# New issue ranks for the steps of an attention and expert kernel

## Chip, cores and metric

The kernel runs on one NeuronCore of a Trainium2 chip. The metric is the device time of one execution in microseconds (us), lower is better. PE is the matmul engine (TensorE), PEld its weight loads, DVE the vector engine, ACT the scalar engine, POOL is GpSimd, SP the engine that issues most transfers.

## The reference, cut to what matters

```python
# q, k, v: (8 batches, 8 heads, 576, 64) float32
q_d, k_d, v_d = means of q, k, v over groups of 4 positions       # 144 pooled positions
out_up    = repeat(softmax(q_d k_d^T / 8) v_d, 4)                  # pooled attention, every query
out_local = softmax(q k^T / 8, only where |i - j| < 4) v           # local attention
x = (out_up + out_local) as (4608 tokens, 512)
logits = x @ w_gate                                                # 8 experts
# pairs (token, expert) are taken in order of falling logit; a token goes to the first
# expert that still has room (576 tokens each)
for e in range(8):
    out[tokens of e] = relu(x[tokens of e] @ w1[e]) @ w2[e]        # 512 -> 1024 -> 512
```

## The kernel before

The program has two parts, the attention (class `Attention`, from L60) and the experts with their routing (classes `Experts` and `Routing`). Neither is a plain loop. Each part is cut into streams, and each stream is a Python generator whose pieces between two `yield`s are called steps. A planner (class `Plan`) always runs the step with the lowest rank among the next steps of all streams; a step that needs an event which no step has given yet first runs the stream that gives it. What a step runs is appended to the program, so the order of steps is the order of instructions on every engine, and each engine works through its own instructions in that order. The ranks come from a table, `KEYS` (L1484), with one list per stream and one number per step; the two parts share the table and each has its own sequence, 1947 steps for the attention (ranks 0 to 1946) and 1641 for the experts (0 to 1640). The last number of most lists belongs to the empty end of a stream.

The attention's streams, with the batch or unit as the last number of their names:

- `Nq0`, `Nk0`, `Nv0` and so on (`load`, L155): SP loads a batch's q, k or v, 1 MB, in one transfer (two halves for batch 0) into one of six buffers. `Nt` loads the last 16 pooled groups of q and k (two transfers of 128 KB, one buffer, so batch b waits until batch b-1 has been read by step `Q`), `Nw` the same of v (waits until POOL has summed the batch before).
- `Rq000` to `Rk117` (`trw`, L291): PE transposes a quarter of a batch's q or k (L300), ACT or DVE copies it out of the accumulator (L279 and L277 are the helper's lines). `Q0` (`trt`, L323) does the tail groups (L333).
- `Gq00`, `Gk20` (`gsum`, L248): sums over groups of four for the pooled attention, on POOL, for batch 0 on DVE (L266, L269). `U0` (`gsum_v`, L224): the same for v on POOL (L234 to L243).
- `B00` (`down_s`, L354): pooled scores on PE (L362, L365), then maximum and difference on DVE and the exponential on ACT. `C00` (`down_t`, L391): transposes of these weights on PE and the copy out on ACT (L410). `E00` (`down_v`, L414): the products with v and the division; `E1` also writes them to HBM.
- `S_0` to `S_35` (`loc_s`, L487): local scores of four windows of 32 queries (L505, L511), softmax on DVE, ACT and, for the last scaling, POOL (L536). `T_0` (`loc_t`, L540): transposes of these weights (L546) and the copy out on ACT (L554). `W_0` loads the windows of v, `P_0` the pooled result, `V_0` (`loc_v`, L559) multiplies (L569) and copies the rows of x out, `D_0` stores them, `X_0` (`logits`, L591) computes the gate's logits of 128 tokens.
- `F0`, `F1` clear buffers; `F0` also has 13 matmuls that nothing uses. `Z0`, `Z1` prepare the first routing.

The experts' streams, with k, the turn of the expert, as the number: `S` and `R` are the routing of turn k (a chain of small DVE operations and small matmuls that finds the tokens), `L` loads its weights (four transfers of 1 MB on SP, L1283), `W` splits them into two 16-bit parts (a cast on ACT, L1298, and a difference on DVE, L1303; eight pieces of three steps), `G` gathers its tokens' rows (POOL, L1326), `X` splits these and transposes them by DMA (L1367), `H` is the first product on PE (32 steps of 6 matmuls, L1394), `E` the relu (L1422, L1426), `C` the second product (40 steps of 3 matmuls of 512 columns, L1449, in five chunks of eight steps, with two accumulators `pX` in turn) and `Y` the scaling on ACT (L1468) and the scatter to the output (POOL, L1473). A chunk of `C` waits until `Y` has read the chunk two before. Matmuls at L795 and L1340 compute nothing that is used.

Of the kernel before, what the change touches and what calls it, by code (L numbers as in the profile page):

```python
# [1246 lines left out]
class Experts:  # L1247
# [237 lines left out]
    "B00": [48, 52, 67, 69, 546],  # L1485
    "B01": [223, 224, 233, 245, 246],
    "B02": [309, 314, 323, 348, 360],
    "B03": [545, 564, 573, 593, 630],
    "B04": [769, 778, 792, 825, 1726],
    "B05": [1013, 1020, 1047, 1048, 1078],  # L1490
    "B06": [1327, 1329, 1339, 1428, 1431],
    "B07": [1565, 1566, 1573, 1595, 1924],
    "B10": [78, 89, 90, 96, 112],
    "B11": [234, 244, 251, 280, 288],
    "B12": [370, 378, 383, 392, 709],
    "B13": [566, 578, 580, 586, 588],
    "B14": [859, 864, 868, 869, 871],
    "B15": [1052, 1062, 1077, 1112, 1243],
    "B16": [1387, 1390, 1391, 1406, 1522],
    "B17": [1572, 1580, 1589, 1606, 1641],  # L1500
    "B20": [82, 98, 99, 109, 764],
    "B21": [237, 258, 277, 282, 793],
    "B22": [389, 391, 402, 430, 1171],
    "B23": [577, 591, 595, 598, 1911],
    "B24": [875, 897, 910, 917, 1079],
    "B25": [1085, 1091, 1097, 1113, 1277],
    "B26": [1393, 1410, 1412, 1419, 1474],
    "B27": [1579, 1591, 1599, 1614, 1616],
    "C0": [138, 148, 201, 202, 216, 218, 228, 229, 232, 236, 237, 240, 241, 250, 252, 257, 259, 265, 267, 268, 275, 276, 283, 286, 287, 293, 299, 303, 308, 311, 312, 315, 318, 319, 320, 336, 338, 339, 341, 342, 343],
    "C00": [101, 102, 520],  # L1510
    "C01": [305, 321, 1001],
    "C02": [416, 420, 463],
    "C03": [658, 674, 1156],
    "C04": [946, 951, 1374],
    "C05": [1134, 1138, 1306],
    "C06": [1451, 1452, 1462],
    "C07": [1659, 1665, 1746],
    "C1": [386, 399, 400, 417, 437, 438, 447, 448, 454, 464, 470, 471, 474, 476, 483, 486, 491, 494, 496, 507, 511, 516, 518, 521, 527, 528, 533, 536, 540, 541, 546, 548, 553, 554, 555, 565, 570, 576, 577, 578, 579],
    "C10": [125, 128, 429],
    "C11": [331, 337, 585],  # L1520
    "C12": [448, 469, 501],
    "C13": [683, 687, 689],
    "C14": [935, 937, 1517],
    "C15": [1184, 1185, 1885],
    "C16": [1456, 1465, 1631],
    "C17": [1620, 1667, 1841],
    "C2": [604, 632, 647, 669, 670, 674, 678, 679, 694, 695, 704, 705, 715, 716, 720, 721, 723, 729, 730, 734, 735, 738, 742, 747, 750, 754, 755, 758, 760, 761, 767, 769, 781, 782, 783, 784, 794, 795, 796, 797, 798],
    "C20": [116, 117, 133],
    "C21": [304, 310, 312],
    "C22": [457, 462, 786],  # L1530
    "C23": [620, 622, 787],
    "C24": [927, 929, 930],
    "C25": [1126, 1133, 1560],
    "C26": [1448, 1449, 1563],
    "C27": [1656, 1672, 1674],
    "C3": [856, 885, 886, 892, 896, 897, 904, 910, 911, 919, 920, 924, 926, 928, 929, 931, 937, 938, 941, 942, 948, 954, 959, 962, 966, 969, 970, 975, 977, 981, 988, 989, 996, 998, 1000, 1002, 1004, 1007, 1008, 1009, 1010],
    "C30": [118, 122, 126],
    "C31": [294, 296, 332],
    "C32": [483, 485, 1778],
    "C33": [654, 659, 782],  # L1540
    "C34": [940, 941, 1498],
    "C35": [1145, 1149, 1400],
    "C36": [1444, 1447, 1594],
    "C37": [1637, 1646, 1785],
    "C4": [1045, 1093, 1104, 1106, 1111, 1112, 1116, 1123, 1141, 1147, 1148, 1150, 1154, 1155, 1158, 1159, 1166, 1167, 1169, 1173, 1176, 1180, 1181, 1184, 1187, 1192, 1194, 1195, 1196, 1202, 1204, 1210, 1219, 1220, 1222, 1223, 1224, 1225, 1226, 1227, 1229],
    "C5": [1267, 1276, 1278, 1279, 1323, 1325, 1327, 1328, 1331, 1333, 1335, 1336, 1337, 1338, 1339, 1342, 1345, 1346, 1347, 1348, 1353, 1355, 1356, 1357, 1358, 1359, 1360, 1361, 1362, 1363, 1364, 1365, 1368, 1369, 1370, 1371, 1377, 1378, 1380, 1386, 1404],
    "C6": [1413, 1424, 1466, 1468, 1476, 1477, 1478, 1479, 1480, 1481, 1482, 1483, 1489, 1490, 1491, 1499, 1501, 1503, 1504, 1505, 1506, 1507, 1508, 1509, 1513, 1515, 1517, 1520, 1522, 1524, 1525, 1527, 1530, 1531, 1533, 1534, 1535, 1537, 1538, 1539, 1541],
    "C7": [1593, 1594, 1595, 1596, 1597, 1598, 1599, 1600, 1601, 1602, 1603, 1604, 1605, 1606, 1608, 1609, 1611, 1612, 1613, 1614, 1615, 1616, 1617, 1618, 1620, 1621, 1622, 1623, 1624, 1625, 1626, 1627, 1629, 1630, 1631, 1632, 1633, 1634, 1635, 1636, 1640],
    "D_0": [426, 1747],
    "D_1": [403, 1120],  # L1550
    "D_10": [1063, 1322],
    "D_11": [1075, 1698],
    "D_12": [1110, 1618],
    "D_13": [959, 1269],
    "D_14": [1229, 1479],
    "D_15": [1315, 1814],
    "D_16": [1182, 1199],
    "D_17": [1291, 1603],
    "D_18": [1361, 1463],
    "D_19": [1467, 1662],  # L1560
    "D_2": [540, 1738],
    "D_20": [1432, 1476],
    "D_21": [1478, 1615],
    "D_22": [1607, 1925],
    "D_23": [1658, 1839],
    "D_24": [1621, 1675],
    "D_25": [1759, 1897],
    "D_26": [1772, 1834],
    "D_27": [1713, 1865],
    "D_28": [1876, 1928],  # L1570
    "D_29": [1852, 1854],
    "D_3": [671, 1230],
    "D_30": [1843, 1895],
    "D_31": [1860, 1869],
    "D_32": [1898, 1946],
    "D_33": [1919, 1923],
    "D_34": [1881, 1883],
    "D_35": [1921, 1927],
    "D_4": [827, 1418],
    "D_5": [635, 851],  # L1580
    "D_6": [824, 1172],
    "D_7": [780, 1162],
    "D_8": [1014, 1195],
    "D_9": [932, 1002],
    "E0": [121, 124, 128, 140, 145, 157, 166, 172, 180, 187, 194, 203, 208, 222, 230, 231, 235],
    "E00": [148, 150, 151, 164],
    "E01": [341, 343, 358, 397],
    "E02": [511, 512, 513, 680],
    "E03": [694, 699, 701, 722],
    "E04": [965, 969, 970, 971],  # L1590
    "E05": [1204, 1205, 1225, 1399],
    "E06": [1486, 1490, 1492, 1729],
    "E07": [1685, 1686, 1687, 1853],
    "E1": [353, 364, 373, 374, 390, 392, 394, 398, 408, 409, 414, 419, 443, 468, 469, 475, 1329],
    "E10": [152, 154, 155, 156, 157, 158, 159],
    "E11": [342, 362, 365, 367, 368, 376, 395],
    "E12": [529, 549, 551, 554, 559, 603, 604],
    "E13": [761, 762, 763, 772, 800, 801, 806],
    "E14": [988, 1006, 1007, 1008, 1028, 1030, 1239],
    "E15": [1215, 1226, 1228, 1231, 1232, 1256, 1539],  # L1600
    "E16": [1496, 1513, 1514, 1518, 1519, 1521, 1574],
    "E17": [1688, 1701, 1703, 1707, 1708, 1736, 1913],
    "E2": [580, 583, 593, 594, 597, 606, 630, 631, 646, 649, 667, 668, 686, 697, 707, 711, 976],
    "E3": [799, 800, 807, 809, 821, 825, 836, 837, 848, 852, 862, 869, 893, 894, 898, 903, 1161],
    "E4": [1015, 1021, 1025, 1039, 1049, 1057, 1060, 1067, 1072, 1082, 1100, 1103, 1118, 1137, 1144, 1145, 1203],
    "E5": [1232, 1235, 1242, 1243, 1259, 1260, 1263, 1264, 1289, 1290, 1291, 1294, 1299, 1300, 1315, 1317, 1319],
    "E6": [1405, 1406, 1415, 1416, 1417, 1418, 1423, 1425, 1444, 1445, 1451, 1455, 1471, 1472, 1473, 1484, 1485],
    "E7": [1548, 1549, 1554, 1555, 1557, 1558, 1566, 1567, 1573, 1574, 1581, 1582, 1587, 1589, 1590, 1591, 1592],
    "F0": [1, 41],
    "F1": [45, 414],  # L1610
    "G0": [55, 56],
    "G1": [224, 225],
    "G2": [465, 479],
    "G3": [618, 672],
    "G4": [830, 833],
    "G5": [1061, 1168],
    "G6": [1250, 1284],
    "G7": [1427, 1469],
    "Gk00": [43, 51],
    "Gk01": [146, 192],  # L1620
    "Gk02": [250, 269],
    "Gk03": [525, 526],
    "Gk04": [756, 757],
    "Gk05": [934, 936],
    "Gk06": [1275, 1392],
    "Gk07": [1508, 1555],
    "Gk20": [53, 77],
    "Gk21": [186, 214],
    "Gk22": [308, 320],
    "Gk23": [502, 507],  # L1630
    "Gk24": [833, 1353],
    "Gk25": [966, 1190],
    "Gk26": [1301, 1905],
    "Gk27": [1493, 1609],
    "Gq00": [16, 19, 20],
    "Gq01": [123, 130, 303],
    "Gq02": [240, 266, 372],
    "Gq03": [487, 493, 770],
# [519 lines left out]
```

## Time and profile before

| what | value |
|---|---|
| time, median of 3 runs | 694.86 us (691.03 to 695.32) |
| profiled execution: time / span | 698.04 us / 696.40 us |
| PE busy, share of the span | 649.7 us, 93% |
| PEld, DVE, ACT, POOL busy | 468.3, 489.7, 356.0, 252.6 us |
| mean granted clock of PE | 0.990 of full speed |
| attention, routing of the first expert, rest (read from PE's lines) | 0 to 244, 244 to 272, 272 to 696 us |

The span runs from the first to the last instruction of the profiled execution; its time is 1.64 us longer. Busy time of an engine is the union of its instructions; the end of a matmul is modelled. The views used are windows (busy time in given stretches), the chain of waits (followed back from the end), waits (who waited for whom), the timeline of an engine, and groups of instructions by line.

### The profile page before, as it was taken

To read this page: it belongs to the slowest core of one execution; us is meant where nothing else is said; L and a number is where in the kernel's file an instruction comes from. 1 tells how busy PE (TensorE), PEld (TensorE's weight loads), DVE (VectorE), ACT (ScalarE), POOL (GpSimd) and SP (SyncE) were. 2 spreads that over 40 slices of the span, in tenths; PEclk is the share of its full clock that TensorE was granted. 3 is DMA by queue.
4 is the path that set the end of the run, shared out by engine and by line. 5 is a ranking of instruction groups with operands and counts; after the bars stand their busy time and mean duration, and the time that the engine had idled before them with its cause. 6 is when DMAs were issued, how large, how long until landed. Compare 5 with 4: busy or idle time off the path is not lost.

```text
span 696.4 us, 19145 instructions
## 1 busy us (share of the span) xinstructions
PE 649.7 (93%) x7702; PEld 468.3 (67%) x7702; DVE 489.7 (70%) x1408; ACT 356.0 (51%) x711; POOL 252.6 (36%) x330
## 2 busy tenths in 40 slices
PE   6898999899899897998999999989999999999994
PEld 3787789788798866674664665664665764755741
DVE  5888487686777968797998887868986765552300
ACT  5796978968786714334334253234443355342210
POOL 8589747493764305004122131131131212211011
PEclk9999999999999999999999999999999999999997
DMA  9958888868877716339256744624734775431001
GB/s 271 299 124 248 242 235 244 223 195 239 230 197 186 221 40 192 119 126 264 57 207 140 284 129 113 252 82 97 274 92 99 276 216 151 145 60 62 8 32 38
DMA packets 137713, 116.80 MB, mean 168 GB/s; under 512 B 86232, under 2 KB 114392, under 8 KB 137624
## 3 DMA queue, kind: packets, MB, share of 16 engines
q1 hardware_dynamic: 130104, 93.71, 46.3%
q0 software_dynamic: 6512, 21.24, 9.7%
q8 instruction: 61, 1.00, 0.6%
q10 hardware_dynamic: 1008, 0.62, 0.4%
q14 instruction: 28, 0.23, 0.1%
HBM read 86.05 MB, written 21.23 MB: 154 GB/s over the span
## 4 chain that ended last, share of the span: by engine, by line
PE 41%; issue 25%; POOL 11%; DVE 8%; DMA 6%; ACT 6%; SPq 2%; another core or an unknown queue 0%; POOLq 0%; DVEq 0%; ACTq 0%
PE pH L1394 13%; PE pX L1449 13%; POOL out_dram L1473 3%; POOL xg L1326 2%; DMA nat<-in_q_dram 2%; PE o L569 2%; ACT qz L279 2%; DMA x_dram<-x 2%; POOL gtmp L266 2%; PE pR L850 1%; PE g L511 1%; PE g L300 1%; PE pX L795 1%; DMA nat<-in_k_dram 1%; DMA nat<-in_v_dram 1%
## 5 line engine op out<-in xcount | busy, mean ns | idle before, releaser
L1394 PE MATMUL pH<-xt,wh 128*128 128x256 f16 (+1 forms) x1024 | 191.6, 286 | 0.6 <-DVE xt L1354 0.6
L1449 PE MATMUL pX<-wh,ht 128*128 128x512 f16 (+1 forms) x640 | 187.5, 379 | 0.0
L1394 PE MATMUL pH<-xt,wl 128*128 128x320 f16 (+1 forms) x512 | 144.7, 287 | 0.0
L1449 PEld LDWEIGHTS <-ht 128*128 128x128 f16 (+1 forms) x960 | 79.2, 100 | 79.5 <-issue 2.2
L1473 POOL DMA_INDIRECT out_dram<-y,idx x40 | 41.4, 1036 | 213.4 <-ACT y L1468 180.0
L1449 PE MATMUL pX<-wl,ht 128*128 128x512 f16 (+1 forms) x320 | 118.1, 380 | 0.0
L1394 PEld LDWEIGHTS <-wh 128*128 128x128 f16 x1024 | 94.4, 98 | 32.0 <-issue 5.6
L1422 ACT ACTIVATE ht<-pH 128x512 f16<-128x512 f32 (+1 forms) x128 | 45.5, 407 | 136.3 <-PE pH L1394 92.8
L1303 DVE SCALAR_TENSOR_TENSOR wl<-nat,wh 128x512 f16<-128x512 f32 x128 | 84.2, 683 | 12.9 <-ACT wh L1298 12.5
L1426 DVE SCALAR_TENSOR_TENSOR ht<-pH,ht 128x512 f16<-128x512 f32 (+1 forms) x128 | 52.2, 449 | 41.2 <-ACT ht L1422 37.3
L1298 ACT ACTIVATE wh<-nat 128x1024 f16<-128x1024 f32 x64 | 65.9, 1054 | 2.5 <-DMA nat<-in_moe_w_dram 2.5
L1326 POOL DMA_INDIRECT xg<-x_dram,idx x40 | 43.2, 1080 | 62.8 <-DVE idx L1177 33.0
L1468 ACT ACTIVATE y<-pX 128x512 f32<-128x512 f32 (+2 forms) x41 | 23.9, 584 | 79.0 <-PE pX L1449 38.2
L1394 PEld LDWEIGHTS <-wl 128*128 128x128 f16 x512 | 50.1, 98 | 13.0
L554 ACT COPY pt<-g 38x512 f32<-38x512 f32 x72 | 41.7, 579 | 5.4 <-PE g L546 3.4
L569 PE MATMUL o<-vw,pt 128*64 128x64 f32 x1152 | 41.0, 224 | 2.4 <-ACT x L581 1.8
L300 PE MATMUL g<-ident,nat 128*128 128x128 f32 x256 | 36.3, 277 | 7.4 <-DMA nat<-in_q_dram 3.0
L569 PEld LDWEIGHTS o<-vw,pt 128*64 128x64 f32 x1152 | 36.9, 138 | 5.5 <-issue 2.1
L511 PE MATMUL g<-kt,qz 128*64 128x38 f32 x1152 | 40.0, 225 | 0.5 <-ACT kt L279 0.5
L511 PEld LDWEIGHTS g<-kt,qz 128*64 128x64 f32 x1152 | 39.4, 138 | 1.3 <-issue 1.2
L536 POOL TENSOR_TENSOR sw<-sw,rs 128x304 f32<-128x304 f32 x36 | 25.2, 704 | 39.8 <-DVE rs L534 28.2
L266 POOL TENSOR_TENSOR gtmp<-qz 64x576 f32<-64x576 f32 x28 | 32.0, 1143 | 18.5 <-DVE kdt L269 7.3
(234 smaller groups left out, 1145.8 us busy)
## 6 DMA issues: line engine op xcount, KB each, us to landing
nat<-in_moe_w_dram SPq DMA_DIRECT2D x28, 1024.0 KB
vw<-in_v_dram SPq DMA_DIRECT2D x136, 78.0 KB
x_dram<-x SPq DMA_DIRECT2D x36, 256.0 KB
nat<-in_q_dram SPq DMA_DIRECT2D x7, 1024.0 KB
nat<-in_k_dram SPq DMA_DIRECT2D x7, 1024.0 KB
nat<-in_v_dram SPq DMA_DIRECT2D x7, 1024.0 KB
vw<-up_dram SPq DMA_DIRECT2D x36, 64.0 KB
up_dram<-xu SPq DMA_DIRECT2D x8, 256.0 KB
```

Of the source, the lines that this page charges most:

```text
L266: eng.tensor_tensor(tmp.rearrange("p a (w i) -> p a w i", w=NW) if which == "q" else tmp, sv[..., ::2], sv[..., 1::2], op=OP.add)
L300: nc.tensor.transpose(p[:, a, :, fp], src[:, 4 * hh + 2 * a + s, 2 * fp:2 * fp + 2].rearrange("p f d -> p (f d)"), self.ident)
L511: nc.tensor.matmul(sv[64 * a:64 * a + 64, 4 * g + c], self.qz[b % 2][:, 2 * g + a, w].rearrange("p s q -> p (s q)"), self.kt[b][:, 2 * g + ...
L569: nc.tensor.matmul(o[64 * i:64 * i + 64, 64 * (4 * g + h):64 * (4 * g + h) + 64], pt[:, 2 * g + i, h].rearrange("p b q -> p (b q)"), self. ...
L1298: nc.scalar.activation(hi, r, AF.Copy, scale=sc)
L1303: nc.vector.scalar_tensor_tensor(lo[:, a:a + LOP], r[:, a:a + LOP], sc, hi[:, a:a + LOP], op0=OP.mult, op1=OP.subtract)
L1326: self.fetched = self.nc.gpsimd.indirect_dma_start(out=xg[:n], out_offset=None, in_=self.x, in_offset=bass.IndirectOffsetOnAxis(ap=idx[:n, ...
L1394: nc.tensor.matmul(p[:, s, :s1 - s0], self.w[k, d][a][:, 128 * f:128 * f + 128], self.xt[k][:, b, d, s0:s1], start=j == 0, stop=j == len(s ...
L1422: nc.scalar.activation(hi, q, AF.Relu)
L1426: nc.vector.scalar_tensor_tensor(lo, q, 0.0, hi, op0=OP.max, op1=OP.subtract)
L1449: nc.tensor.matmul(p[o:o + m], self.ht[k][:, f, h0:h0 + m], self.w[k, 4 + f // 2][b][:, 512 * (f % 2):512 * (f % 2) + 512], start=j < part ...
L1473: i = nc.gpsimd.indirect_dma_start(out=self.out, in_=y[:n], in_offset=None, out_offset=bass.IndirectOffsetOnAxis(ap=plan.vals["idx", k][:n ...
```

## The change

All lists of `KEYS` are replaced but seven (`G0`, `L0`, `M0`, `R0`, `S0`, `S1`, `G1`); the number of steps in each list is the same, and no other line changes. In the attention the rank of a step moves by 83 in the mean and 37 in the median, in the experts by 12 and 5. The first 99 steps of the experts (the routing of the first expert and the start of its products) keep their ranks. Of the 1126 lines of the diff, these are the ones that the text below speaks of (the new lists follow the old):

```diff
--- before.py
+++ after.py
@@ -1482,568 +1482,568 @@
 ENG = mybir.EngineType
 ORDX = {ENG.PE, ENG.DVE, ENG.Activation, ENG.SP}
 KEYS = {
...
-    "B00": [48, 52, 67, 69, 546],
-    "C05": [1134, 1138, 1306],
-    "C35": [1145, 1149, 1400],
-    "E05": [1204, 1205, 1225, 1399],
-    "Gk00": [43, 51],
-    "H5": [1191, 1201, 1215, 1216, 1228, 1237, 1238, 1239, 1240, 1241, 1245, 1247, 1251, 1253, 1255, 1256, 1262, 1265, 1273, 1274, 1280, 1281, 1282, 1283, 1292, 1293, 1295, 1296, 1297, 1298, 1303, 1306, 1313],
-    "Nk0": [23, 27, 316],
-    "Nk3": [334, 346],
-    "Nk7": [1317, 1318],
-    "Nq0": [7, 11, 647],
-    "Nq5": [734, 738],
-    "Nq7": [1292, 1797],
-    "Nt0": [0, 2],
-    "Nt1": [70, 364],
-    "Nw0": [75, 1003],
-    "Nw2": [333, 555],
-    "Q0": [3, 4, 5, 6, 202],
-    "Q1": [83, 84, 86, 87, 100],
-    "Rk103": [375, 407, 431, 433],
-    "Rq000": [8, 9, 10, 13],
-    "Rq007": [1363, 1369, 1370, 1562],
-    "S_33": [1682, 1722, 1725, 1727, 1730, 1731, 1743, 1766],
-    "T_33": [1771, 1810, 1817, 1877],
-    "W5": [1054, 1066, 1073, 1110, 1117, 1119, 1142, 1153, 1165, 1185, 1199, 1200, 1221, 1246, 1249, 1252, 1254, 1268, 1269, 1271, 1272, 1277, 1285, 1286, 1287],
-    "Y4": [1156, 1175, 1190, 1230, 1231, 1261, 1266],
...
+    "B00": [50, 64, 67, 81, 326],
+    "C05": [1181, 1185, 1722],
+    "C35": [1177, 1182, 1315],
+    "E05": [1211, 1212, 1213, 1261],
+    "Gk00": [42, 130],
+    "H5": [1200, 1226, 1229, 1231, 1232, 1234, 1236, 1238, 1240, 1241, 1243, 1244, 1248, 1261, 1263, 1265, 1266, 1268, 1270, 1271, 1273, 1275, 1278, 1279, 1285, 1290, 1294, 1295, 1300, 1313, 1314, 1316, 1319],
+    "Nk0": [12, 27, 38],
+    "Nk3": [297, 361],
+    "Nk7": [1399, 1821],
+    "Nq0": [2, 26, 1125],
+    "Nq5": [726, 1003],
+    "Nq7": [1116, 1388],
+    "Nt0": [5, 59],
+    "Nt1": [34, 387],
+    "Nw0": [24, 374],
+    "Nw2": [348, 446],
+    "Q0": [8, 11, 15, 16, 23],
+    "Q1": [48, 60, 61, 70, 74],
+    "Rk103": [367, 381, 383, 547],
+    "Rq000": [3, 4, 9, 10],
+    "Rq007": [1237, 1279, 1281, 1403],
+    "S_33": [1694, 1699, 1704, 1705, 1709, 1719, 1738, 1739],
+    "T_33": [1755, 1780, 1795, 1924],
+    "W5": [1058, 1092, 1106, 1137, 1168, 1179, 1193, 1195, 1196, 1197, 1198, 1201, 1202, 1204, 1205, 1206, 1207, 1208, 1209, 1210, 1211, 1212, 1213, 1214, 1215],
+    "Y4": [1142, 1148, 1216, 1217, 1242, 1256, 1262],
...
```

## Rows read from the trace of the kernel before

**Rows 1.** windows: us busy of PE, PEld, DVE, ACT, POOL; clock, DMA share, GB/s

```profile
0.00:25.00 25.00, 18.09 (x195) 12.28 (x195) 16.28 (x32) 14.09 (x25) 16.23 (x23) 1.00 0.96 289
25.00:50.00 25.00, 23.43 (x431) 20.46 (x424) 20.71 (x49) 23.66 (x52) 20.89 (x29) 1.00 0.66 183
50.00:75.00 25.00, 21.65 (x426) 19.55 (x426) 18.46 (x38) 18.95 (x44) 20.92 (x29) 1.00 0.77 226
75.00:200.00 125.00, 116.00 (x2360) 105.59 (x2359) 87.97 (x219) 104.33 (x216) 80.89 (x113) 1.00 0.81 229
200.00:244.00 44.00, 41.25 (x936) 37.52 (x935) 37.65 (x100) 30.23 (x61) 19.54 (x42) 1.00 0.71 203
244.00:272.00 28.00, 25.15 (x288) 18.98 (x284) 18.84 (x82) 7.50 (x11) 4.71 (x7) 0.94 0.32 105
272.00:440.00 168.00, 161.19 (x1305) 101.17 (x1305) 143.03 (x480) 66.60 (x131) 37.85 (x39) 0.99 0.51 155
440.00:470.00 30.00, 27.41 (x249) 20.20 (x246) 23.91 (x73) 11.15 (x24) 8.37 (x9) 1.00 0.56 193
470.00:690.00 220.00, 215.49 (x1536) 132.50 (x1533) 122.84 (x342) 79.48 (x151) 43.16 (x42) 1.00 0.42 123
```

**Rows 2.** chain of waits, 376 to 379 us: start, length, what

```profile
377.24 1.32 PE pX L1449 x6
```

**Rows 3.** timeline of PE, 324 to 463 us: start, length, what, idle before

```profile
325.39 0.31 PE L850 MATMUL pR<-oh,cmp 128*128 128x64 bf16 x5 [1.74 <-DVE thr L833]
...
459.00 0.16 PE L890 MATMUL pR<-un,nohead 128*128 128x1 bf16 x1 [1.52 <-DVE un L877]
...
461.71 0.31 PE L850 MATMUL pR<-oh,cmp 128*128 128x64 bf16 x5 [1.07 <-DVE cmp L808]
```

**Rows 4.** timeline of the SP queue, first 10 us

```profile
0.88 0.69 SPq L167 DMA_DIRECT2D natt<-in_q_dram  x1
1.63 0.57 SPq L167 DMA_DIRECT2D natt<-in_k_dram  x1
2.25 1.13 SPq L195 DMA_DIRECT2D nat<-in_q_dram  x2
```

**Rows 5.** timeline of PE, 8 to 27 us

```profile
9.40 1.09 PE L300 MATMUL g<-ident,nat 128*128 128x128 f32 x8 [1.47 <-DMA nat<-in_q_dram]
...
18.46 0.97 PE L362 MATMUL g<-kdt,qdz 128*128 128x144 f32 x6 [1.99 <-DVE kdt L269]
...
25.20 1.16 PE L333 MATMUL g<-ident,natt 128*64 128x64 f32 x32
```

**Rows 6.** chain of waits, 55 to 67 us

```profile
57.75 0.33 POOL gtv L242
58.08 0.16 SPq L178
...
58.29 6.74 DMA nat<-in_k_dram
...
65.16 0.63 PE g L300 x4
```

**Rows 7.** chain of waits, 176 to 190 us

```profile
178.40 8.05 DMA nat<-in_q_dram
```

**Rows 8.** timeline of PE, 186 to 188 us

```profile
186.58 0.63 PE L300 MATMUL g<-ident,nat 128*128 128x128 f32 x4 [1.16 <-DMA nat<-in_q_dram]
```

**Rows 9.** groups of instructions: busy us, mean ns of one, idle before

```profile
L1298 ACT ACTIVATE wh<-nat 128x1024 f16<-128x1024 f32 x64 | 65.9, 1054 | 2.5 <-DMA nat<-in_moe_w_dram 2.5
...
L266 POOL TENSOR_TENSOR gtmp<-qz 64x576 f32<-64x576 f32 x28 | 32.0, 1143 | 18.5 <-DVE kdt L269 7.3 <-ACT qz L349 5.9 <-DVE qz L277 2.6
...
L410 ACT COPY ptd<-g 128x384 f32<-128x384 f32 (+1 forms) x32 | 13.9, 455 | 1.2 <-PE g L402 0.5 <-PE g L398 0.3
```

**Rows 10.** timeline of PE, 225 to 232 us

```profile
230.29 0.66 PE L546 MATMUL g<-ident,sw 128*128 128x128 f32 x4 [1.24 <-POOL sw L536]
```

**Rows 11.** timeline of DVE, 316 to 330 us

```profile
324.63 0.21 DVE L833 SCALAR_TENSOR_TENSOR thr<-pR,tabs 128x49 int16<-128x49 f32 x1 [2.15 <-remote]
```

1060 rows, old and new, of the table KEYS are left out of this document.

## The prediction

> **What bounds the kernel now.** I read the windows by stretch first, then what PE waits for, then the timelines where it waits. The reader is to see three parts in [rows 1]. In the attention (0 to 244 us) PE is busy 18.09 + 23.43 + 21.65 + 116.00 + 41.25 = 220.4 us, so 23.6 us are idle; a fourth to a third of that lies in the first 25 us, and ACT is close behind (23.66 of 25 us in the second stretch) and POOL too (20.89 and 20.92). From 244 to 272 the routing of the first expert runs as a chain, with PE partly busy on filling matmuls. From 272 on PE is the engine that sets the end: 161.19 of 168, 27.41 of 30, and 215.49 of 220, of which the last 4 us or so are the tail after the last matmul. The work there is dense: six products of 512 columns hold PE for 1.32 us [rows 2], 0.22 us each, at a granted clock of 1.00, the level of 2.4 GHz. An order of issue removes none of that work. So only idle PE time can be won: some 23.6 us in the attention, and behind it three waits of 1.74, 1.52 and 1.07 us [rows 3].
>
> The profiled execution took 698.04 us: a span of 696.40 and 1.64 around it. It is 3.2 us slower than the median of the runs shown (694.86). I form the change as a difference on the profiled execution and take it from the median.
>
> **How I read the tables.** Every step of every stream keeps its content; only its rank changes. No instruction is added or removed. For a wait, what counts is how much PE work is issued between the step that starts something and the step that needs it. I sum PE's steps in rank order, each at the time its matmuls hold PE in the timeline where nothing is waited for (a transposing step 0.5 us, the two score steps of a unit 1.0 together, its value steps 1.0, and so on), and call the sum before a step its place. All attention steps come to 219 us, which agrees with the 220.4 busy; a place unit is then 244/219 = 1.11 us of time. Steps on other engines stand at the PE work ranked before them.
>
> **Part by part.**
> *The first 25 us.* Before, SP issues the two small tail loads, then q [rows 4], and PE waits 1.47 us until q lands at 9.40; later it waits 1.99 us for DVE's group sums before the first pooled score step at 18.46 [rows 5]. After, the first half of q is issued first, 1.37 us earlier by these rows (0.88 against 2.25), with 256 KB less before it (0.9 us at the 289 GB/s of this stretch); PE transposes q, then takes the tail step, and the first half of k stands before the second half of q. The tail step of batch 1 (Q1, 1.16 us at 25.20 before [rows 5]) moves ahead of that pooled score step (B00), so the sums of DVE get cover. Best case both waits go, 3.5 us. Worst case Q1's load, which SP can issue only once Q0 has read the only buffer, lands no sooner than q did from its issue (9.40 - 2.25 = 7.2 us): issued near 11 us, it lands at 18, PE waits as long as before, and nothing but the order has changed, or half a microsecond is lost. Only its two 128 KB pieces are then in the queue, so I go nearer to the good end: -2.0 (from -3.5 to +0.5).
>
> *The third batch's k.* On the chain, POOL's value sum ends at 58.08, SP then issues the small value load (L178) that waited for it and behind it the 1 MB of k at 58.29; k takes 6.74 us and PE starts at 65.16 after 1.51 us idle [rows 6]. The new table issues that k (Nk3, rank 297) before that value load (Nw2, 374), and from the load to its first use there are 7.9 us of PE work instead of 5.3; 7.9 x 1.11 = 8.8 us is over 6.74. The wait goes: -1.5.
>
> *The last batch's q and k.* q was issued at 178.40 and took 8.05 us [rows 7] for 8.1 us of PE work behind it; PE waited 1.16 us [rows 8]. Now it is ranked 13.0 us of work ahead (14.4 us): -1.2. Against this, k of the same batch goes from 10.8 to 6.4 of work ahead, and q of the sixth from 10.2 to 4.8. One load of before stood 5.2 ahead (k of the sixth batch) and PE waited for no load there, since SP ran ahead of its rank; another with 5.3 cost 1.5. So each may cost 0 to 2.7 us (8.05 - 4.8 x 1.11); I take +1.3 for both together. The net for loads is -1.4 with the part above (from -2.7 to +1.5).
>
> *POOL between 25 and 75 us.* POOL's pooling steps cost 1.14 us for the first add alone [rows 9], 2.0 with the two behind it. Summed in rank order, the POOL work issued before PE's place 40 falls from 42 to 33 us, and before place 60 from 60 to 53. PE idles 25 - 23.43 + 25 - 21.65 = 4.9 us there, 1.5 of it the k above. Some of the rest is POOL's; but ACT, nearly full in the first half of it, gets no less to do. I take -1.0 (from -2.5 to +0.5).
>
> *The end of the attention.* At 230.29 PE idles 1.24 us for POOL's scaled weights of unit 33 [rows 10]. The work between its scores and its transposes (S_33 to T_33) grows from 3.9 to 5.6 us, 1.7 more than before: -1.2. The last unit's steps (scores, transposes, values, logits) end in the same order, and the routing that follows has the same ranks up to 98.
>
> *Waits that the new table tightens.* The transposed pooled weights (C3) must pass ACT, 0.46 us a copy [rows 9], before E0 uses them. That distance falls in the median from 1.9 to 1.3, twice to 0.5 (batches 0 and 5). With the copy and a few tenths of handing over, 0.5 is short by some 0.4. From pooled scores to their transposes the lowest distance falls from 4.3 to 2.9. I take +1.5 for all of these (0 to +3).
>
> *The experts.* The order of large products and routing steps is shuffled by a median of 5 ranks; the first 99 steps are the same, as is the tail's. The three waits [rows 3] sum to 4.3 us; before the first of them DVE had itself waited 2.15 us for something the profile cannot name [rows 11], so another order need not cure it. I take 0 (from -3 to +3).
>
> Sum: -2.0 - 1.4 - 1.0 - 1.2 + 1.5 + 0 = **-4.1 us**. The profiled execution would take 698.04 - 4.1 = 693.9; from the median, **690.8 us**, 0.6% faster.
>
> **Rivals.**
> *The attention closes much further.* For it: POOL leads instead of trailing, and the new places respect landings that the trace shows. If half of the 23.6 us idle goes, 11.8 us, the time is 683. Against it: the waits I can name with their new places sum to about 6. The Trainium skill ("Perfetto Trace Analysis", section "Identifying the Most-Contended Engine") says that matmul busy time is a bad measure of headroom and weight-load busy should be read. By that, estimated from [rows 1], the attention has 244 - 195.4 = 48.6 us to win instead of 23.6, and half of it would give 670. The trace speaks for the matmul row here: the sum of work that PE must hold comes to 219.
>
> *ACT takes over.* A wait removed at one place comes back as a wait for ACT, which has the same work and is within 1.4 us of full in one stretch. The named gains then shrink to the q and k loads: about 694.
>
> *Slower: a run of splits in the sixth expert.* For k=5 the new table ranks the last six of the eight weight splits (W5.6 to W5.23) in one run directly ahead of the store step Y4.2, on ACT and DVE. On ACT these are six casts of 1.05 us [rows 9], 6.3 us. Y4.2 frees the accumulator that PE's step C4.32 needs, and 5.9 us of PE work stand between C4.23, which fills it, and C4.32. ACT casts ahead of PE as long as the weights are there, and then this costs nothing. The last two casts read the fourth transfer, ranked 15.7 us of PE work before C4.32. It must land 13.6 us after its place at the latest (15.7 less two casts); with the 8.05 us that 1 MB took in [rows 7], SP must not be held for more than 5.5 us before it. If SP is held until PE is at C4.32, Y4.2 comes 8.05 + 2.1 = 10.2 us later and PE stands for it: 701. Against it: ACT is busy for only 79.48 of the last 220 us [rows 1] and SP has little else to issue there.
>
> **How the numbers follow.** Chances: forecast 0.43, closes further 0.23, ACT takes over 0.20, slower 0.14. About 1% (6.9 us) is what a measurement can tell here. Of the forecast's cases a quarter (gains over 6.9 us, the good ends above) count as faster: 0.23 + 0.11 = 0.34 faster; 0.32 + 0.20 less 0.01 = 0.51 within 1%; 0.15 slower. The term bounds put the forecast's own range at 684 to 696; with the cases beside it I give 682 to 699.
>
> **What would show it.** Right: PE's first transposes before 9 us; no wait over 1 us for k of batch 3 or q of batch 7; no idle before T_33; the attention ended near 240 instead of 244; from the first routing step to the end the same 452 us within 3. Wrong: the attention unchanged in length with waits now on ACT; a PE gap of several us near the last third of the experts with ACT's casts before a store; or an expert stretch that moved by more than 3 us.

## The result: 1.0% slower, with one long stall late in the experts

The changed kernel takes 700.64 us (median of 13 runs, 697.18 to 707.47) beside 694.86 us of the kernel before in the same session: ratio 1.0104, 95% interval 1.0073 to 1.0136. The forecast was 690.8 with 699 as its upper end. The profiled execution took 699.13 us, a span of 697.5. The two profiled executions are only 1.1 us apart (699.13 and 698.04) where the medians are 5.8 apart, because that of the kernel before was 3.2 us over its median: the two traces show where PE stands, but less than the whole loss.

The windows of the changed kernel, in the columns of [rows 1]:

```profile
0.00:25.00 25.00, 19.89 (x242) 14.40 (x243) 17.54 (x34) 16.88 (x33) 16.15 (x23) 1.00 0.99 301
25.00:50.00 25.00, 23.21 (x383) 19.13 (x382) 19.93 (x46) 21.98 (x48) 18.90 (x27) 1.00 0.76 207
50.00:75.00 25.00, 22.43 (x437) 19.57 (x435) 17.20 (x37) 20.07 (x42) 21.01 (x28) 1.00 0.81 219
75.00:200.00 125.00, 117.75 (x2430) 107.29 (x2426) 92.28 (x231) 104.24 (x218) 85.09 (x119) 1.00 0.85 236
...
272.00:440.00 168.00, 164.44 (x1352) 104.42 (x1353) 145.85 (x493) 67.84 (x134) 37.75 (x40) 1.00 0.55 168
440.00:470.00 30.00, 29.89 (x256) 19.71 (x254) 24.69 (x82) 13.53 (x28) 7.62 (x8) 1.00 0.41 122
470.00:690.00 220.00, 206.76 (x1460) 127.82 (x1458) 113.43 (x308) 73.19 (x140) 41.72 (x41) 0.98 0.45 119
575.00:600.00 25.00, 14.68 (x94) 8.93 (x93) 1.07 (x3) 2.43 (x6) 3.13 (x4) 0.80 0.76 104
```

PE is busier than in [rows 1] in five of these stretches up to 470 us and less busy in one (23.21 against 23.43). From 470 to 690 it loses 215.49 - 206.76 = 8.7 us, and the last row shows where: of 25 us from 575 on, PE works 14.68, at a mean clock of 0.80. The page's list of the costliest groups names the cause in one line (busy, mean ns of one, idle before, and what ended it):

```profile
L1394 PE MATMUL pH<-xt,wh 128*128 128x256 f16 (+1 forms) x1024 | 193.4, 288 | 11.0 <-DMA xt<-xs 10.3
```

Of the 11.0 us that PE ever waited at this line, one wait is 10.3. The timeline of PE has it, and the places of [rows 5] and [rows 10] too:

```profile
6.56 1.04 PE L300 MATMUL g<-ident,nat 128*128 128x128 f32 x8
...
9.38 1.09 PE L300 MATMUL g<-ident,nat 128*128 128x128 f32 x8 [0.69 <-DMA nat<-in_k_dram]
...
17.73 0.66 PE L511 MATMUL g<-kt,qz 128*64 128x38 f32 x16 [0.96 <-ACT kt L279]
...
230.88 0.66 PE L546 MATMUL g<-ident,sw 128*128 128x128 f32 x4 [0.28 <-POOL sw L536]
...
591.71 0.69 PE L1394 MATMUL pH<-xt,wh 128*128 128x320 f16 x2 [10.32 <-DMA xt<-xs]
```

The last row is step H6.2, the first that reads tokens 256 to 575 of turn 6 (the seventh expert). These tokens come from the third to fifth of X6's five transposes by DMA. The kernel before has no wait there:

```profile
593.15 0.44 PE L1394 MATMUL pH<-xt,wh 128*128 128x320 f16 x2
```

In the changed kernel the granted clock is 0.5, the level of 1.2 GHz, from 587 to 597 us: two matmuls of 320 columns take 0.69 us after the wait, where the same pair takes 0.43 us from 597 us on, at the other level.

What SP's queue issues there (start, length, what), in the changed kernel:

```profile
566.25 2.84 SPq L1367 DMA_TRANSPOSE xt<-xs  x2
569.36 0.38 SPq L1283 DMA_DIRECT2D nat<-in_moe_w_dram  x1
569.84 14.91 SPq L1367 DMA_TRANSPOSE xt<-xs  x3
```

and in the kernel before:

```profile
569.81 6.73 SPq L1367 DMA_TRANSPOSE xt<-xs  x5
```

The new table ranks the last weight load of turn 7 (L7.3, 1 MB) between the second transpose and the third, and the three behind it take 14.91 us to issue. At the same time POOL issues turn 7's gather, first and last of its five pieces:

```profile
566.45 1.15 POOL L1326 DMA_INDIRECT xg<-x_dram,idx  x1 [5.12 <-DVE xs L1364]
...
575.51 0.92 POOL L1326 DMA_INDIRECT xg<-x_dram,idx  x1 [0.30 <-issue]
```

In the kernel before the first piece goes out long after the transposes, when DVE has written the list of rows:

```profile
594.73 1.30 POOL L1326 DMA_INDIRECT xg<-x_dram,idx  x1 [3.29 <-DVE idx L1177]
```

The transposes' inputs were not late: DVE ended the last of X6's five differences (L1364) at 572.85, 19 us before the wait's end. So three theories stood. A: L7.3 ahead of them in SP's queue holds the transposes. B: turn 7's gather, in flight beside them, slows them. C: something further up makes them late.

### The profile page after: what moved, and what is told of

Read it like the earlier page. It is cut to its first block, busy times and chain, and to the rows that moved or that the text cites. A ratio compares the mean times of both kernels' runs of the same rounds, so it can differ in the third digit from the quotient of the medians.

```text
span 697.5 us, 19146 instructions
## 1 busy us (share of the span) xinstructions
PE 649.2 (93%) x7702; PEld 467.8 (67%) x7702; DVE 488.8 (70%) x1408; ACT 355.3 (51%) x711; POOL 253.8 (36%) x330
## 3 DMA queue, kind: packets, MB, share of 16 engines
q0 software_dynamic: 6512, 21.24, 10.3%
## 4 chain that ended last, share of the span: by engine, by line
PE 51%; issue 17%; DVE 13%; ACT 7%; POOL 6%; DMA 3%; POOLq 0%; SPq 0%; ACTq 0%; DVEq 0%
PE pH L1394 17%; PE pX L1449 17%; PE g L511 2%; DMA vw<-up_dram 2%; POOL out_dram L1473 2%; ACT qz L279 2%; PE o L569 2%; PE g L300 2%; ACT kt L279 1%; PE g L546 1%; POOL gtmp L266 1%; PE pR L850 1%; PE g L599 1%; DVE wl L1303 1%; PE g L362 1%
## 5 line engine op out<-in xcount | busy, mean ns | idle before, releaser
L1394 PE MATMUL pH<-xt,wh 128*128 128x256 f16 (+1 forms) x1024 | 193.4, 288 | 11.0 <-DMA xt<-xs 10.3
L1473 POOL DMA_INDIRECT out_dram<-y,idx x40 | 43.0, 1075 | 209.1 <-ACT y L1468 173.4
L1468 ACT ACTIVATE y<-pX 128x512 f32<-128x512 f32 (+2 forms) x41 | 23.7, 584 | 62.5 <-PE pX L1449 29.8
```

The lines of the kernel that those rows point to most:

```text
L1394: nc.tensor.matmul(p[:, s, :s1 - s0], self.w[k, d][a][:, 128 * f:128 * f + 128], self.xt[k][:, b, d, s0:s1], start=j == 0, stop=j == len(s ...
L1473: i = nc.gpsimd.indirect_dma_start(out=self.out, in_=y[:n], in_offset=None, out_offset=bass.IndirectOffsetOnAxis(ap=plan.vals["idx", k][:n ...
```

## Experiments

The kernel before took 694.86, 697.26, 695.16 and 700.91 us (medians) in the four sessions, so kernels are compared by their ratio to it. The first session has the changed kernel, the second the three moves (e_load_back, e_gather_back, e_both_back) and e_attn_new, the third after_again, e_exp_new and e_before_gather, the fourth the other three. "Attention" is the time of the first routing matmul (L850), "rest" the span from there to the end; both are read from one profiled execution of each kernel, and the rest of one and the same kernel differs by 2 to 7 us between two executions.

| kernel | ratio, interval | attention | rest | wait before H6.2 |
|---|---|---|---|---|
| before | 1 | 244.3 | 452.1 | none |
| changed | 1.0104 (1.0073 to 1.0136) | 239.9 | 457.6 | 10.32 |
| after_again, the changed kernel again | 1.0167 (1.012 to 1.0214) | 239.5 | 464.8 | 9.93 |
| e_exp_new, only the experts' table new | 1.0221 (1.0173 to 1.0269) | 246.1 | 464.2 | 7.81 |
| e_attn_new, only the attention's table new | 0.9928 (0.9886 to 0.9969) | 243.7 | 449.3 | none |
| e_attn_again, the same | 0.9919 (0.988 to 0.9958) | 242.7 | 451.0 | none |
| e_load_back, the changed kernel with the load moved | 1.0023 (0.9983 to 1.0063) | 239.4 | 455.2 | 2.98 |
| e_gather_back, with the gather moved | 1.0022 (0.9981 to 1.0064) | 241.4 | 455.6 | 1.97 |
| e_both_back, with both moved | 0.9998 (0.9956 to 1.0039) | 242.7 | 452.6 | none |
| e_both_again, the same | 0.9965 (0.993 to 1.0) | 241.7 | 456.5 | none |
| e_both_slack, both moved and one routing step later | 0.9967 (0.9935 to 0.9998) | 238.8 | 453.2 | none |
| e_before_gather, the kernel before with the gather early | 0.9996 (0.9963 to 1.003) | 248.3 | 447.9 | none |

**The two halves apart.** The table of the kernel before, with the new lists of the attention's streams alone:

> The table of the changed kernel for the attention and that of the kernel before for the experts. If the new attention order is worth what its trace shows (first routing matmul 4.4 us earlier) and nothing of it is given back later: 690 to 691 us, ratio 0.993 to 0.995. If the experts' old order takes back what the attention gave (loads or clock behind it): 693 to 696 us.

and of the experts' streams alone:

> The table of the kernel before for the attention and that of the changed kernel for the experts. If the two halves add up (changed kernel 1.0104, attention alone 0.9928): ratio 1.014 to 1.021, with the stall of 8 to 10 us before the second half of H6. If the loss comes from what the new attention leaves behind it: ratio 0.998 to 1.006.

The attention's half is worth 0.7 to 0.8%, some 5 us, and nothing takes it back. The experts' half costs 2.2%. The product of the two, 0.9928 x 1.0221 = 1.015, lies in the interval of the changed kernel when it is run again (1.0167), and above that of its first session (1.0104). Its stall moves with the experts' half; there the ratio is a little over the forecast and the wait a little under it:

```profile
604.39 0.69 PE L1394 MATMUL pH<-xt,wh 128*128 128x320 f16 x2 [7.81 <-DMA xt<-xs]
```

> The changed kernel itself, once more. If the stall before the second half of H6 is a property of its order: PE idles 8 us or more there again, and the ratio to the kernel before is 1.007 to 1.014. If it was one execution's bad luck: under 3 us of idle time there, with the loss elsewhere, in the waits of the routing steps that the three kernels with moved steps show (1 to 3 us each on L867 and L890).

The stall is a property of the order, since it is there again at the same matmul in another execution:

```profile
598.44 0.69 PE L1394 MATMUL pH<-xt,wh 128*128 128x320 f16 x2 [9.93 <-DMA xt<-xs]
```

The ratio, 1.0167, is over the 1.014 expected: this execution has the stall and the routing wait too (L890, below), which the expectation had as alternatives.

**The load moved back.** In the changed kernel:

```diff
-    "L7": [1287, 1312, 1321, 1349, 1350],
+    "L7": [1287, 1312, 1321, 1381.3, 1381.4],
```

> The changed kernel, with one step moved: the last weight load of the eighth expert (1 MB, SP) goes behind the five transposes of the seventh expert's tokens instead of between the second and the third. Theory A (the load ahead of them in SP's queue holds the transposes): the idle time of PE before the first matmul on the second half of the tokens, 10.32 us in the changed kernel's trace, falls under 1 us, the clock stays up behind it, and the time comes to 687 to 690 us. Theory B (the gather of the eighth expert's rows, in flight beside the transposes, slows them): the transposes start some 5 us earlier but still take over 10 us, 3 to 7 us of the idle time stay, and the time is 693 to 698 us. Theory C (the transposes' inputs are late): no change, 700 us.

**The gather moved back.** The list of rows of turn 7 and with it the gather (by rank between H6.5 and H6.6; the expectation's H6.7 is a slip):

```diff
-    "R7": [1286, 1296, 1297, 1299, 1301, 1303, 1327, 1331],
+    "R7": [1286, 1296, 1297, 1299, 1301, 1303, 1327, 1400.4],
-    "G7": [1387, 1482],
+    "G7": [1400.5, 1482],
```

> The changed kernel, with the last step of the eighth expert's routing (its list of rows, which lets POOL issue the gather) moved behind the seventh expert's H6.7, so that the gather of the eighth expert's rows starts after the seventh expert's transposes; the weight load stays between them. Theory A (the weight load): the idle time before the second half of H6 stays at 8 us or more, 697 to 700 us. Theory B (the gather): the three transposes behind the load take about 5 us instead of 15, the idle time falls under 2 us, 687 to 691 us. Theory C: no change, 700 us.

**Both moved back.**

> The changed kernel with both moves, the weight load behind the transposes and the list of rows (so the gather) behind H6.7. Theories A and B: no idle time over 1 us before the second half of H6, the clock near 1.0 there, 686 to 690 us, and the same as the better one of the two single moves unless both are needed. Theory C (inputs late): the idle time stays, 699 to 701 us.

The waits before H6.2 in the timelines of PE, first the kernel with the load moved:

```profile
591.40 0.43 PE L1394 MATMUL pH<-xt,wh 128*128 128x320 f16 x2 [2.98 <-DMA xt<-xs]
```

then the one with the gather moved:

```profile
593.75 0.43 PE L1394 MATMUL pH<-xt,wh 128*128 128x320 f16 x2 [1.97 <-DMA xt<-xs]
```

and the window of the one with both, where PE is busy throughout at full clock:

```profile
575.00:600.00 25.00, 25.00 (x165) 14.49 (x162) 11.44 (x25) 10.23 (x18) 9.60 (x9) 1.00 0.95 219
```

Theory C falls as the cause of the stall: each single move takes 7 to 8 us of the stall away. A and B are both true, and neither alone. Each single move also keeps the clock up (both rows above have 0.43 us a pair). With the load moved, the wait that stays (2.98 us) is at the lower end of what B had forecast (3 to 7 us) and not under 1 us, as A had it. With the gather moved it fell under 2 us, as B said, but the three transposes behind the load took until 592, not 5 us: the gather that now starts at 586.18 still met the last of them. The times are misses where a theory that holds had 686 to 691: 697.96 us with the gather moved and 697.74 with both, some 7 us over; with the load moved it is 698.22, at the upper end of B's 693 to 698. Some 2 us of that is the session, whose kernel before took 697.26, and a part of the rest is a second loss in the new experts, shown below.

The packets of the five transposes (4608 of 256 bytes in each kernel, 1.18 MB) give the sizes. Counted from the trace's packets, first to last, and in the last column of numbers from the end of the last of X6's differences on DVE (the last input) to the last packet:

```
kernel             first    last   us  after last input  in flight beside them
before            571.02  577.78   6.8   4.9   nothing
e_attn_new        567.61  574.35   6.7   4.9   nothing
e_attn_again      568.29  575.06   6.8   4.9   nothing
e_before_gather   572.35  581.77   9.4   8.2   gather
e_both_slack      574.17  583.91   9.7   3.5   end of an earlier load (L7.2), stores
e_both_again      580.34  590.10   9.8   3.5   the same
e_both_back       577.36  589.12  11.8   5.5   the same, more of that load
e_gather_back     577.05  592.05  15.0   8.8   load L7.3, stores, then the gather's start
e_load_back       574.67  590.66  16.0  10.8   gather, stores
e_exp_new         582.65  603.78  21.1  15.7   load, gather, stores
after_again       574.59  597.77  23.2  17.8   load, gather, stores
changed           567.47  591.15  23.7  18.3   load, gather, stores
```

In the old order the transposes have the engines to themselves: 1.18 MB in 6.8 us are 174 GB/s. In the changed kernel they share them with L7.3, the gather and three stores (L1473), and get 50 GB/s. The first column of times is not company alone: in the old order DVE makes the five inputs within 3.1 to 3.8 us, in the new one within 7.2 to 8.7, and a transpose can't start before its input. So a part of the longer times is theory C's, but it does not explain the stall: in the changed kernel the last input is ready 18.3 us before the last packet. The stores, which no run moved, don't hold the transposes by themselves: with both moves 174 packets of 4 KB still go out for them in e_both_slack, and the transposes end 3.5 us after their last input.

In the trace of the changed kernel 30 to 260 of the transposes' packets start per us from 580 to 590 us, while gather and stores are in flight, and 923 in the us after these have ended. The gather suffers as well: its five pieces take 14.2 us to land in the median, against 3.7 over the whole kernel. The packets of POOL's queue are 12 times as large, 1.97 MB in 608 packets beside the transposes, 3.2 KB each. The Trainium skill ("DMA: Bandwidth & Descriptors", section "Queues, rings and completion order") says that each DMA engine takes turns between the queues that have work, a packet at a time, and that such a packet typically holds some 9 to 17 descriptors. That would leave small packets little of an engine's time, and the trace agrees so far that they fall to a fifth of their rate (141 packets per us from 580 to 590, where 4608 in 6.8 us are 680). Between 583 and 584 us 131 of the transposes' packets start beside 23 of POOL's queue; whether what the trace counts as a packet is one in the sense of that rule no run shows, so the numbers neither bear it out nor refute it. Sharing of bytes is not the whole of it either: all queues together moved 178 GB/s in the changed kernel's 23.7 us, less than in e_load_back (195), e_gather_back (236) and e_before_gather (257), and from 578 to 580 us the DMA engines were busy for a quarter of the time, at 38 GB/s, with the transposes unfinished. Why both are so slow together is not settled.

**The gather alone, put into the kernel before.**

```diff
-    "R7": [1257, 1258, 1275, 1326, 1343, 1381, 1390, 1394],
+    "R7": [1257, 1258, 1275, 1286.5, 1290.5, 1294.5, 1299.5, 1299.6],
-    "G7": [1427, 1469],
+    "G7": [1299.7, 1469],
```

> The kernel before with the eighth expert's last routing steps and its gather placed ahead of the seventh expert's transposes, so that the five gathers go out beside the five transposes, with no weight load between them. Theory B (the gather slows them): the five transposes take over 11 us from the first one's issue to the last packet, where the kernel before has 8; those ahead of H6 have 10 us or more in hand, so the time moves by less than 2 us (ratio 0.998 to 1.004). Theory A (the load alone): the transposes take 7 to 9 us as before.

SP's queue in that kernel:

```profile
571.14 8.83 SPq L1367 DMA_TRANSPOSE xt<-xs  x5
```

From the first issue to the last packet 581.77 - 571.14 = 10.6 us, where before it was 577.78 - 569.81 = 8.0. That is 2.7 us more, just short of the 11 that B had named and over the 9 of A; here the inputs come as close together as in the kernel before (3.1 us), and what differs beside the transposes is the gather. The end of the attention (248.3 here) has nothing to do with it, and the ratio is 1, as expected: the transposes have room ahead of H6.

**What is left in the new experts.** With both moves the stall is gone and 8 to 12 us are back (rest 452.6 and 456.5 against 464.8). But the kernel with the new attention and the old experts is still 0.5 to 0.7% faster. In all six traces of the new experts' order after the first session (the changed kernel again, the new experts alone, the moves) PE idles 2.2 to 3.1 us at one more place, which the changed kernel's first trace doesn't have. From the changed kernel run again, all engines, 502 to 507 us:

```profile
502.93 0.17 PE L867 MATMUL pR<-cs,rep 128*128 128x8 f16 x1
...
506.54 0.71 ACT L1422 ACTIVATE ht<-pH 128x512 f16<-128x512 f32 x2 [5.84 <-remote]
506.58 0.17 DVE L877 TENSOR_TENSOR_SCAN un<-cap,pR 128x8 bf16<-128x8 f32 x1 [3.87 <-remote]
506.80 0.16 PE L890 MATMUL pR<-un,nohead 128*128 128x1 bf16 x1 [3.02 <-DVE un L877]
```

It is a round trip of the routing, second level of R6: PE's L867, DVE's scan L877, PE's L890. PE's matmul is recorded at 502.93, but ACT and DVE, which both wait for PE's count, move 3.6 us later (2.8 to 3.7 in the six), and the profile finds nothing that released them ("remote", as in [rows 11]; in e_gather_back it names PE's L889 for the scan, which had ended 2 us earlier). In the changed kernel's first trace the scan starts 0.23 us after that matmul. In two of the six the wait also costs clock: in e_both_again, after 3.06 us, the granted clock is 0.5 from 512.5 to 515.9 us, and in e_exp_new, after 2.95 us, from 514.3 to 517.7, while in after_again, after 3.02 us, it stays at 1.00. The next kernel has both moves and puts PE's step with L889 and L890 (R6.11) two H steps later:

```diff
-    "R6": [..., 1071, 1072, 1075, 1081, ...],
+    "R6": [..., 1071, 1072, 1077.5, 1081, ...],
```

> The changed kernel with both moves (weight load and list of rows back), and two H steps of the fifth expert more between PE's L867 and the pair L889/L890 of the sixth routing turn's second level, where PE idles about 3 us in every kernel with the new experts' order of these sessions. Theory D (the reply of DVE is late, and PE has too little else to do): the 1.5 us of matmuls moved into the wait cut it by 1.5 us, to 1.0 to 1.5 us, ratio to the kernel before 0.996 to 0.999. Theory E (PE itself makes no progress there, so that its counts come late whatever stands in between): the idle time stays within 0.5 us, at the same matmul or behind it, ratio as with the two moves alone.

> The changed kernel with both moves, again, beside the two others on one chip. No idle time over 1 us ahead of the second half of H6; ratio to the kernel before 0.996 to 1.001.

> The new table for the attention alone, again, beside the two others on one chip: ratio 0.991 to 0.995, and 0.3 to 0.8 per cent under the changed kernel with both moves, whose experts keep the waits on L867 and L890.

PE's timeline with the two steps in between:

```profile
503.65 0.17 PE L867 MATMUL pR<-cs,rep 128*128 128x8 f16 x1
505.80 0.17 PE L889 MATMUL pR<-one,head 128*128 128x1 bf16 x1
507.58 0.16 PE L890 MATMUL pR<-un,nohead 128*128 128x1 bf16 x1 [1.61 <-DVE un L877]
509.54 0.31 PE L850 MATMUL pR<-oh,cmp 128*128 128x64 bf16 x5 [0.96 <-DVE cmp L808]
```

PE goes on through the steps put in between, which speaks against the mechanism of E. The wait is 1.4 us shorter, as D says, but the next step of the chain (L850) now waits 0.96, and the ratio is the same as with the two moves alone (0.9967 and 0.9965). D's range for the ratio holds 0.9967, but the gain it was to show against the two moves alone did not come, since the scan still starts 3.71 us after L867 and what is behind it moves along; and the two waits together, 2.57 us against 3.06, are within the 0.5 us that E had named. So this run does not decide between the two. Why PE's count comes so late at this place, in some executions and not in others, stays open.

The best version is the new attention with the old experts: 0.9928 and 0.9919, faster than either kernel.

## Why the prediction was wrong

**The attention came as forecast, and a little better.** First routing matmul at 239.9 instead of 244.3 (-4.4; the sum forecast was -4.1 with the experts at 0). Over all traces it is 241.1 in nine with the new order and 246.2 in three with the old. By its steps, from the idle time of PE in each window against [rows 1]:

- The first 25 us: forecast -2.0, idle 6.91 to 5.11, -1.8. PE transposes at 6.56, before the 9 us named; the two waits of [rows 5] became five of 0.33 to 1.03 us.
- k of the third batch and POOL, 25 to 75 us: forecast -1.5 and -1.0, idle 4.92 to 4.36, -0.6. The wait for k is gone, but at 55.29 PE waits 1.01 us for POOL's value sums (L243), where the forecast had counted on less POOL work in front. This term was mis-sized.
- 75 to 200 us: forecast -1.2 for q of the last batch, +1.3 for the two tightened loads, +1.5 for the tightened copies, together +1.6; idle 9.00 to 7.25, -1.75. No load of q or k keeps PE waiting over 1 us, so the +1.3 was nothing. New waits came (1.52 us at 154.06 for the load of the pooled result, 1.47 at 89.41 for POOL, 1.25 at 180.11 for ACT) and were outweighed. The tightened terms were mis-sized too, the other way.
- The last unit: forecast -1.2; the wait of [rows 10] went from 1.24 to 0.28, -1.0.

That the sum of these came out is in part luck: the second line is 1.9 us worse than forecast and the third 3.4 better.

**The step that failed is the experts' term, "I take 0 (from -3 to +3)".** It cost +13 to +17 us in the later sessions: the rest took 464.2 and 464.8 against 447.9, 449.3 and 451.0. Of that, 7.8 and 9.9 us are the wait before H6.2, 3.0 in each the wait at L890, and an estimated 2.5 the 5 us of work at half clock behind the stall. In the first session's traces it was +5.5 (457.6 against 452.1), since there the three waits of [rows 3], 4.3 us, did not appear in the changed kernel and the second loss (L890) did not either; by that session's medians it was some 11 (5.8 lost in all, and the attention's 5 besides). The term was argued from how little the ranks moved, a median of 5, and the slower rival from one run of splits (turn 5), which did not come. Nothing was summed over the queues: three streams, each moved by a few dozen ranks, put a load, a gather and five transposes into the same 20 us. The prediction did not apply its rule for loads, PE work between issue and use, to the experts; by that rule H6.2 would have looked safe: its transposes were issued 15 us before PE came to it (566.25 to 581.4), and they had taken 8.0 from issue to the last packet. The rule takes the landing time from a row where the transfer was alone, and that is what is wrong with it: here the landing time depends on what else the table puts beside the transfer, and first to last packet went from 6.8 to 23.7 us.

**The range.** The bounds of the terms, added as they stand, reach from 682 to 702 us (694.86 - 12.9 and + 7.3), not from 684 to 696, and 700.64 is inside the first and outside the second. The stall was in no term all the same: the experts' +3 is far under it.

**The marks named.** Four of the right ones came: transposes before 9 us, no long wait for k of batch 3 or q of batch 7, hardly any idle time before T_33, the attention's end near 240. The fifth failed: the experts' stretch moved by more than 3 us, named as the sign of a wrong forecast. The gap stood at the seventh expert, with transfers, not ACT's casts, in front of it.

**The rivals.** Half of the attention's idle time did not go: of 23.6 us about 5 went, so the estimate of 670 by the rule of the Trainium skill ("Perfetto Trace Analysis", section "Identifying the Most-Contended Engine") did not come. Which of the two measures is nearer to what could be won, one order does not show: 5 us is far from half of either. ACT did not take over: the idle time of the attention shrank in spite of new waits for it. The slower rival had the right side and size (701) at a wrong place, with a wrong mechanism; that its number came out is luck.

## What to carry to other kernels

When an order is searched with landing times from a trace, each landing time holds only for the traffic that was beside it. For a moved transfer, list everything that all queues (SP's and POOL's) have in flight between its issue and its use in the new order, and take the landing time from a row with the same company, or keep such transfers apart. The one to protect is the one that PE needs next, here five transposes in small packets; the gather beside them was slowed as much, but nothing waited for it yet. And try the halves of a change apart: here one half alone is the gain.

## What the runs showed of the hardware that was not expected

- Five transposes by DMA, 1.18 MB together, take 6.7 to 6.8 us alone, 9.4 beside a gather, 15 to 16 with either a 1 MB load or a gather beside them in the new order, and 21 to 24 with both. After their last input it is 4.9 us alone, 8.2 to 10.8 beside one of them, and 15.7 to 18.3 beside both.
- After PE had stood for 10.3 us, its granted clock was 0.5 from 587 to 597 us, 5 us of the wait and 5 us of the work behind it; in the window from 575 to 600 it was 0.80 in the mean. After waits of 2 to 3 us at the same place it stayed at full speed; after waits of about 3 us at L890 it was 0.5 for a stretch in two executions (2.95 and 3.06 us) and stayed at 1.00 in another (3.02).
- At one matmul of the routing (L867 of R6) the scan on DVE that waits for it started 2.8 to 3.7 us after the matmul in seven traces of the new experts' order, and 0.23 us after it in the first.
